# Five token tiles of a linear-attention and MLP kernel, set to other addresses in SBUF

## The chip, the cores and the metric

One core of one Trainium2 chip runs the whole kernel. The metric is device time in microseconds of one execution; the kernel before was run three times, and the median counts.

## What is computed

Linear attention on 4 x 8 heads of 576 tokens, then a gated MLP with an RMS norm ahead of it, then a second MLP. The weights come in as 64-bit floats.

```python
def phi(x):                                   # random features, 128 of them
    h = einsum('bhsd,md->bhsm', x, omega) - sum(x * x, -1) / 2
    return exp(h - max(h, -1)) / sqrt(m)
q_p, k_p = phi(q * scale), phi(k * scale)
kv, z = einsum('bhsm,bhsd->bhmd', k_p, v), sum(k_p, axis=2)
x = einsum('bhsm,bhmd->bhsd', q_p, kv) / (einsum('bhsm,bhm->bhs', q_p, z) + 1e-6)
# (2304 tokens, 512)
xn = x / sqrt(mean(x * x, -1) + 1e-6) * rms_g
g = xn @ w_gate                               # 512 x 1536
x = (g * sigmoid(g) * (xn @ w_val)) @ w_out   # 1536 x 512
h = x @ w2_in                                 # 512 x 2048
return (h * sigmoid(h)) @ w2_out              # 2048 x 512
```

## The kernel before

**Tiles.** The 2304 tokens are 18 tiles of 128, taken in five blocks: four long ones of 512 tokens and a short one of 256 (`blocks`, L58). Block `j` has one token tile `xs[j]` (L91): for each of the 128 partitions, two halves (a high and a low part of each number, in fp32r) times four chunks of the 512 features times the block's tokens. A weight tile holds, in the same manner, a high and a low half of 512 columns. Every product is made of three passes (`PASS`, L236): high by high, high by low, low by high. `part` (L247) issues the matmuls of one product of a token block: 12 of them, with a weight slice of 128 columns as the stationary operand and a slice of `xs[j]` (512 or 256 columns) as the moving one. Its line is L250. Each matmul has a weight load of its own, which the trace lists as engine PEld.

**Order.** In the attention stage (up to about 190 us) a list written out by hand, `ORDER`, sets the order of all operations; it holds the first products of blocks 0 to 2, too (L250 into tiles named b, and L1067). After that `stream` (L357) runs eleven sweeps over the hidden columns, five of the first MLP and six of the second. In each sweep every block has its L250 products (tiles named g), and between them stand the products of the block ahead of it that lead back to 512 features: L304 in the first MLP (a weight slice stationary, the hidden tile `h` moving), L337 in the second (`h` stationary, a weight tile moving), both into tiles named y. So long g work and long y work take turns, and once in each sweep the short block comes in between.

**Addresses.** Tiles are laid out in SBUF one behind the other: constants, the five `xs` tiles, `ya`, weight tiles, and the rest, with another group of weight tiles at the far end (padded by `EDGE` elements, L185). A weight tile has 4,096 bytes in each partition, a long `xs` tile 16,384, a hidden tile 4,096 or 2,048. All of these are whole multiples of 512 bytes, and so all the weight tiles, hidden tiles and long token tiles begin at one and the same address modulo 512 (it is 192). The slices that a matmul takes are also multiples of 512 bytes into a tile. The word **offset** is used below for the moving operand's address less the stationary one's, modulo 512 bytes. Before, it is 0 for all L304 and L337 matmuls and for L250 of the long blocks, and 64 for L250 of the short block, whose tile is shifted by `SHIFT` = 16 elements of 4 bytes inside a longer buffer. In the attention stage L661 (the feature projection, `hl` stationary and `bd` moving, 256 columns) runs at offsets 384 and 416, as the buffers happen to lie.

**Others that touch the token tiles.** ScalarE and VectorE write them in the attention stage (L908, L956, L961), and in the fifth sweep, between the two MLPs, L317 and L294 write them anew.

Of the kernel before, what the change touches and what calls it, by code (L numbers as in the profile page):

```python
# [9 lines left out]
F32R = mybir.dt.float32r  # L10
# [10 lines left out]
def kernel(  # L21
# [20 lines left out]
    P = 128  # L42
    G = 4
    KC = DM // P
    TB = 4
    EDGE, SHIFT = 72, 16
    scale = 1.0 / float(D) ** 0.25
    half = -0.5 * scale * scale
    eps_den = 1e-6 * M
# [9 lines left out]
    NB, NE = len(blocks), 3  # L59
    tidx = {t: i for i, t in enumerate(tiles)}  # L60

    def out_rows(i):
# [10 lines left out]
    big = ctx.enter_context(tc.tile_pool(name="big", bufs=1))  # L73
# [14 lines left out]
    g_sb = const.tile([P, KC], F32)  # L88
    mhalf = const.tile([P, 1], F32)

    xs = [  # L91
        big.tile([P, 2 * KC * n + (0 if n == TB * P else 8 * SHIFT)], F32R, name=f"xs{j}")
        [:, (0 if n == TB * P else SHIFT):][:, 0:2 * KC * n].rearrange("p (a c n) -> p a c n", a=2, c=KC)
        for j, n in enumerate(blocks)
    ]
    ya = [big.tile([P, KC * blocks[j]], F32, name=f"ya{j}") for j in range(NE)]
# [9 lines left out]
    f = 0  # L106
# [4 lines left out]
    f = 0  # L111
# [978 lines left out]
    with tc.manual_schedule():  # L1090
# [62 lines left out]
        n = 0  # L1153
        for j in range(NE):
            n = add_block(j, sweeps[0][1], n)
# [52 lines left out]
```

## Time and profile before

| | |
|---|---|
| Median of three runs | 982.45 us (981.73 to 982.59) |
| Span of the profiled execution | 980.8 us |
| TensorE busy (PE) | 973.2 us, 99% of the span |
| VectorE, ScalarE, GpSimd busy | 59%, 40%, 30% |
| Chain that ended last | PE 96% |

The page gives the profiled execution's span, from its first to its last instruction, and no other total for it; the median of the runs is 1.7 us above it. TensorE is busy nearly all the time, and the chain of waits that ended last is nearly all its matmuls. The mean duration that the trace gives a matmul holds some 163 ns in which the next one is already streaming, so durations do not add up. What adds up is the time from one start to the next; the chain shows it, since a piece of the chain is a run of matmuls with its length and count.

### The profile page before, as it was taken

Reading aid. Unit: us, or ns where it says so; the run is one execution under the profiler, and the core shown is the slowest. Engines: PE = TensorE matmul, PEld = TensorE weight load, DVE = VectorE, ACT = ScalarE, POOL = GpSimd, SP = SyncE. Lnnn points to the kernel's source line nnn. Section 1 sums busy time; section 2 is a strip of 40 time slices with the busy share of each in tenths; the row PEclk is TensorE's granted clock in tenths of the full one; section 3 lists DMA queues with packets and bytes.
Section 4 is the critical chain, followed back from the end, with each engine's and each line's share of the span. In section 5 each row is a group of like instructions: output and inputs, shape, how many; then the busy total and the mean of one; then the engine's idle time right before and its main releaser. Section 6 shows DMA issues by size and latency. Waiting matters only on the chain.

```text
span 980.8 us, 15407 instructions
## 1 busy us (share of the span) xinstructions
PE 973.2 (99%) x5938; PEld 828.0 (84%) x5938; DVE 575.8 (59%) x1186; ACT 392.5 (40%) x904; POOL 291.3 (30%) x308
## 2 busy tenths in 40 slices
PE   9999999999999999999999999999999999999998
PEld 8989888888888888888898888888888888888887
DVE  7999999886532366774234873615634735435634
ACT  7999777753311123341113334443223223222221
POOL 8877653453310033341001322402402302202200
PEclk9999999999999999999999999999999999999999
DMA  8645443222200012221000111201101101100023
GB/s 197 161 103 139 122 115 114 73 88 74 77 22 1 1 43 65 87 86 44 1 1 22 56 54 43 65 22 43 65 22 43 65 22 43 43 1 22 22 86 108
DMA packets 79481, 60.31 MB, mean 61 GB/s; under 512 B 27312, under 2 KB 73648, under 8 KB 79408
## 3 DMA queue, kind: packets, MB, share of 16 engines
q1 hardware_dynamic: 79136, 59.26, 20.5%
q8 instruction: 47, 0.77, 0.3%
q14 instruction: 26, 0.21, 0.1%
q10 hardware_dynamic: 272, 0.07, 0.0%
HBM read 49.87 MB, written 4.72 MB: 56 GB/s over the span
## 4 chain that ended last, share of the span: by engine, by line
PE 96%; DVE 2%; ACT 1%; DMA 1%; issue 0%; POOL 0%; SPq 0%; ACTq 0%; DVEq 0%; POOLq 0%
PE g L250 46%; PE y L337 20%; PE y L304 13%; PE b L661 5%; PE b L250 3%; PE b L843 2%; PE kv L739 2%; PE b L1067 2%; PE b L632 1%; PE b L947 1%; PE b L819 1%; DVE small L678 0%; DMA x<-in_k_dram 0%; SPq L799 0%; ACT m L176 0%
## 5 line engine op out<-in xcount | busy, mean ns | idle before, releaser
L250 PE MATMUL g<-xs,w 128*128 128x512 f32 (+1 forms) x2256 | 468.0, 366 | 0.0
L250 PEld LDWEIGHTS g<-xs,w 128*128 128x128 f32 x2256 | 391.1, 188 | 70.1
L168 POOL TENSOR_TENSOR m<-m,raw 128x512 int32<-128x512 int32 x136 | 188.5, 1387 | 580.0 <-issue 415.4
L244 DVE TENSOR_TENSOR h<-s,h 128x512 fp32r<-128x512 f32 (+1 forms) x134 | 96.7, 722 | 185.2 <-ACT h L243 185.2
L337 PE MATMUL y<-w,h 128*128 128x512 f32 (+1 forms) x870 | 200.8, 388 | 0.0
L337 PEld LDWEIGHTS y<-w,h 128*128 128x128 f32 x870 | 162.2, 188 | 33.3
L243 ACT ACTIVATE h<-s 128x512 fp32r<-128x512 f32 (+1 forms) x134 | 78.7, 588 | 180.2 <-DVE s L273 158.2
L304 PE MATMUL y<-h,w 128*128 128x512 f32 (+1 forms) x648 | 135.5, 366 | 0.2 <-DVE h L244 0.2
L304 PEld LDWEIGHTS y<-h,w 128*128 128x128 f32 x648 | 112.2, 189 | 20.2 <-DVE h L244 0.4
L284 ACT ACTIVATE s<-g 128x512 f32<-128x512 f32 (+1 forms) x80 | 44.4, 556 | 171.1 <-PE g L250 171.0
L348 DVE TENSOR_TENSOR ya<-y,ya 128x512 f32<-128x512 f32 (+1 forms) x91 | 62.1, 683 | 57.9 <-PE y L337 56.6
L315 DVE TENSOR_TENSOR ya<-y,ya 128x512 f32<-128x512 f32 (+1 forms) x80 | 50.3, 635 | 58.3 <-PE y L304 58.1
L709 ACT ACTIVATE e<-b,nb 128x128 f32<-128x128 f32 x272 | 75.7, 401 | 14.0 <-DVE nb L691 5.4
L273 DVE TENSOR_TENSOR s<-s,g 128x512 f32<-128x512 f32 (+1 forms) x54 | 33.8, 626 | 77.5 <-PE g L250 76.1
L191 ACT ACTIVATE w<-m 128x512 fp32r<-128x512 f32 x68 | 42.8, 630 | 68.7 <-POOL m L168 67.5
L661 PE MATMUL b<-bd,hl 128*128 128x256 f32 x432 | 62.4, 289 | 0.7 <-DVE xt L870 0.5
L661 PEld LDWEIGHTS b<-bd,hl 128*128 128x128 f32 x432 | 55.1, 188 | 4.1 <-ACT e L709 0.8
L194 DVE TENSOR_TENSOR w<-m,w 128x512 fp32r<-128x512 f32 x68 | 53.9, 792 | 2.1 <-ACT w L191 1.9
L267 ACT ACTIVATE s<-g 128x512 f32<-128x512 f32 (+1 forms) x54 | 29.5, 546 | 59.0 <-PE g L250 58.9
L678 DVE TENSOR_REDUCE small<-b 128x4 f32<-128x512 f32 x72 | 49.8, 691 | 4.4 <-PE b L661 2.5
L585 POOL TENSOR_TENSOR sq<-sq 128x256 f32<-128x256 f32 (+2 forms) x80 | 45.7, 584 | 2.4
L581 POOL TENSOR_TENSOR sq<-x 128x512 f32<-128x512 f32 (+1 forms) x40 | 38.1, 959 | 27.3 <-DVE ns L594 10.6
(75 smaller groups left out, 725.5 us busy)
## 6 DMA issues: line engine op xcount, KB each, us to landing
raw<-in_moe_w_out_dram SPq DMA_DIRECT2D x28, 512.0 KB, 3.5
raw<-in_moe_w_in_dram SPq DMA_DIRECT2D x16, 512.0 KB, 3.7
raw<-in_moe_w_gate_dram SPq DMA_DIRECT2D x12, 512.0 KB, 3.7
raw<-in_moe_w_val_dram SPq DMA_DIRECT2D x12, 512.0 KB, 3.5
qT<-e SPq DMA_DIRECT2D x72, 64.0 KB, 2.2
x<-in_k_dram SPq DMA_DIRECT2D x16, 256.0 KB, 3.7
va<-in_v_dram SPq DMA_DIRECT2D x32, 128.0 KB, 4.0
x<-in_q_dram SPq DMA_DIRECT2D x16, 256.0 KB, 3.5
```

The lines of the kernel that those rows point to most:

```text
L168: tt(out=mi, in0=mi, in1=(low if step == 5 else high).bitcast(I32), op=ALU.add)
L194: nc.vector.tensor_tensor(out=st.t[:, 1, :], in0=st.m.bitcast(F32), in1=st.t[:, 0, :].bitcast(F32), op=ALU.subtract)
L243: nc.scalar.activation(out=ht[:, 0, :], in_=s, func=AF.Copy)
L244: nc.vector.tensor_tensor(out=ht[:, 1, :], in0=s, in1=ht[:, 0, :].bitcast(F32), op=ALU.subtract)
L250: nc.tensor.matmul(out=ps, lhsT=w[:, a, cc * P:(cc + 1) * P], rhs=xs[j][:, c, cc, :], start=(n == 0), stop=(n == 3 * KC - 1),)
L304: nc.tensor.matmul(out=ps, lhsT=wt[1, "o", f][:, a, d * P:(d + 1) * P], rhs=hs[f][:, c, :], start=(n == 0), stop=(n == nn - 1),)
L315: nc.vector.tensor_tensor(out=y[:, d, :], in0=ps, in1=y[:, d, :], op=ALU.add)
L337: nc.tensor.matmul(out=ps, lhsT=hs[f][:, a, t * P:(t + 1) * P], rhs=wt[2, "p", f][:, c, d0:d1], start=(n == 0), stop=(n == nn - 1),)
L348: nc.vector.tensor_tensor(out=o[:, t, d0:d1], in0=ps, in1=o[:, t, d0:d1], op=ALU.add)
L661: nc.tensor.matmul(out=st.ps[r][:, 2 * j:2 * j + 2, :].rearrange("p h m -> p (h m)"), lhsT=st.hl[:, c, 2 * r + j, :], rhs=bd[:, a, :], sta ...
L678: nc.vector.tensor_reduce(out=st.mx[:, G * r:G * r + G], in_=st.ps[r], axis=AX.X, op=ALU.max)
L709: nc.scalar.activation(out=st.e[r][:, :, h, :] if blocks4 else st.e[r][:, h, :], in_=src.rearrange("p (a f) -> p a f", a=4) if blocks4 els ...
```

## The change

Each token tile gets a lead of its own, in elements of 4 bytes: 16, 32, 16, 48 and 48. Since the tiles lie one behind the other, the leads add up: the long tiles come to lie 64, 192, 256 and 448 bytes past the weight tiles' address modulo 512, and the short one 640, which is 128. A tail of 96 elements behind the short tile brings the sum to 1,024 bytes, where there were 512 before; so all that lies behind the token tiles moves by 512 bytes and keeps its address modulo 512, and the weight tiles at the far end do not move at all. The offset of L250 is now 64, 192, 256 and 448 in blocks 0 to 3 and 128 in block 4. The offsets of L304, L337, L661 and L1067 stay as they were. No instruction is added, removed or moved: on each engine the list of instructions is the same row by row.

```diff
-    EDGE, SHIFT = 72, 16
+    EDGE = 72
...
+    LEAD, REST = (16, 32, 16, 48, 48), 96
     xs = [
-        big.tile([P, 2 * KC * n + (0 if n == TB * P else 8 * SHIFT)], F32R, name=f"xs{j}")
-        [:, (0 if n == TB * P else SHIFT):][:, 0:2 * KC * n].rearrange("p (a c n) -> p a c n", a=2, c=KC)
+        big.tile([P, 2 * KC * n + LEAD[j] + (REST if j == NB - 1 else 0)], F32R, name=f"xs{j}")
+        [:, LEAD[j]:][:, 0:2 * KC * n].rearrange("p (a c n) -> p a c n", a=2, c=KC)
         for j, n in enumerate(blocks)
     ]
```

## Rows read from the trace of the kernel before

**Rows 1.** The page: span, busy time by engine, granted clock, chain by engine and line.
```profile
span 980.8 us, 15407 instructions
PE 973.2 (99%) x5938; PEld 828.0 (84%) x5938; DVE 575.8 (59%) x1186; ACT 392.5 (40%) x904; POOL 291.3 (30%) x308
...
PEclk9999999999999999999999999999999999999999
...
PE 96%; DVE 2%; ACT 1%; DMA 1%; issue 0%; POOL 0%; SPq 0%; ACTq 0%; DVEq 0%; POOLq 0%
PE g L250 46%; PE y L337 20%; PE y L304 13%; PE b L661 5%; PE b L250 3%; PE b L843 2%; PE kv L739 2%; PE b L1067 2%; PE b L632 1%; PE b L947 1%; PE b L819 1%; DVE small L678 0%; DMA x<-in_k_dram 0%; SPq L799 0%; ACT m L176 0%
```
**Rows 2.** Groups of PE instructions by shape: busy us, mean ns | idle before.
```profile
L250 PE MATMUL g<-xs,w 128*128 128x512 f32 x1776 | 411.4, 389 | 0.0
L337 PE MATMUL y<-w,h 128*128 128x512 f32 x858 | 199.4, 389 | 0.0
L304 PE MATMUL y<-h,w 128*128 128x512 f32 x504 | 117.2, 389 | 0.0
L661 PE MATMUL b<-bd,hl 128*128 128x256 f32 x432 | 62.4, 289 | 0.7 <-DVE xt L870 0.5
L250 PE MATMUL g<-xs,w 128*128 128x256 f32 x480 | 59.8, 280 | 0.0
L250 PE MATMUL b<-xs,w 128*128 128x512 f32 x144 | 37.7, 399 | 0.4 <-DVE w L194 0.4
...
L304 PE MATMUL y<-h,w 128*128 128x256 f32 x144 | 18.3, 283 | 0.2 <-DVE h L244 0.2
```
**Rows 3.** Chain, 217 to 304 us: start us, length us, what. Long blocks alone.
```profile
217.36 16.35 PE g L250 x72
233.71 8.16 PE y L304 x36
241.87 16.32 PE g L250 x72
258.19 8.16 PE y L304 x36
```
**Rows 4.** Granted clock in such a stretch: PE busy (count), PEclk, DMA share, GB/s.
```profile
220.00:300.00 80.00, 80.00 (x355) 1.00 0.17 53
```
**Rows 5.** Chain, the short block's 256-column matmuls: L250 at offset 64, L304 at 0.
```profile
315.93 4.71 PE g L250 x40
...
324.82 3.12 PE y L304 x26
```
**Rows 6.** Chain, the seven long matmuls behind a short block.
```profile
307.26 1.62 PE y L304 x7
```
**Rows 7.** Chain, 640 to 800 us: long y work behind long and behind short g work.
```profile
701.34 8.16 PE y L337 x36
709.50 8.27 PE g L250 x48
717.76 8.20 PE y L337 x36
```
**Rows 8.** Chain, attention stage: L250 at offset 0, L661 at 384.
```profile
137.78 2.77 PE b L250 x12
...
151.18 1.43 PE b L661 x12
```
**Rows 9.** The token tiles' writers behind 189 us: count, duration ns min/median/max, first to last.
```profile
L317 ACT ACTIVATE xs<-ya x20: 417/632/635, 525.9 to 588.7; 128x512 fp32r<-128x512 f32 x16, 128x256 fp32r<-128x256 f32 x4
L294 DVE TENSOR_TENSOR xs<-ya,xs x20: 411/682/1161, 527.2 to 589.1; 128x512 fp32r<-128x512 f32 x16, 128x256 fp32r<-128x256 f32 x4
```

## The prediction, made before the changed kernel ran

> **What bounds the kernel now.** The page comes first: TensorE is busy 973.2 us of a span of 980.8, and the chain that ended last is 96% TensorE; L250 alone has 46% of it as g and 3% as b [rows 1]. The list of groups shows no idle time worth a name ahead of the matmuls of the sweeps [rows 2]. So the span is the sum of the times from one matmul's start to the next, and a change that moves no instruction counts only if it changes these. The groups' mean durations cannot be added, so I read the chain: a run of matmuls, its length and its count.
>
> In a long stretch, 72 matmuls of L250 take 16.32 us, 226.7 ns each, and the L304 matmuls next to them the same, 8.16 by 36 [rows 3]. The clock is granted in full there, 1.00 [rows 4], which is the 2.4 GHz level; 512 columns at 2.4 GHz would be 213.3 ns, so each long matmul carries 13.3 ns on top of its columns. In the short block there are two cases side by side with 256 columns, 106.7 ns: L304 at offset 0 takes 3.12 us by 26, 120.0 ns, and L250 at offset 64 takes 4.71 by 40, 117.8 ns [rows 5]. The surcharge is thus 13.3 ns at offset 0 whether the matmul is long or short, and 11.1 at offset 64. It belongs to the matmul with its weight load, not to the columns, and the address has a part in it. The same difference stands in the mean durations, 283 against 280 [rows 2].
>
> One more thing is to be seen in the chain, and it weighs more for me. The long matmuls' 226.7 ns is a steady rhythm, and they are dearer whenever they are out of it. Right behind a short block seven long matmuls take 1.62 us, 231.4 each [rows 6]. The whole piece of 36 then takes 8.20 where one behind long work takes 8.16 [rows 7]. In the attention stage, where other work cuts in all the time, twelve of L250 in a row take 2.77 us, 230.8 each [rows 8], and that group's mean duration is 399 against 389 [rows 2]. With 256 columns it is the other way about: the steady 120.0 at offset 0 is the dear one, and L661, cut up all the time and at offset 384, runs 1.43 by 12, 119.2 [rows 8].
>
> **The change part by part.** *Long tiles, offset 0 to 64, 192, 256 and 448.* This concerns 1776 matmuls of the sweeps [rows 2], 432 in each of blocks 0 to 2 and 480 in block 3; the 144 of the attention stage are out of rhythm already [rows 2, 8], and I take nothing for them. The trace has no long matmul at any offset but 0, so this cost is bounded. From above: the offset keeps the stream out of its cheap rhythm all the time, at the 230.8 to 231.4 that it shows when out of it [rows 6, 8], which is 4.1 to 4.7 ns more; 1776 x 4.2 = +7.5 us, 1776 x 4.7 = +8.3 us. From below: the long matmul gains what the short one has at 64 against 0, 2.2 ns [rows 5], 1776 x 2.2 = -3.9 us. Far below that, the whole surcharge of 13.3 ns goes, -23.6 us. I take +7.5, from the row of 512 columns and the longer run of the two (the twelve of L250), and not the gain of the 256-column rows. My reason: a 256-column matmul gives its weight load about as much time as its columns need, a long one twice that, and rows 6 and 8 show the two to differ in sign when the rhythm is disturbed.
>
> *Turns between g and y.* Now a turn from long g work to long y work costs nothing, 8.16 behind long and 8.20 behind short work [rows 7], both pairs of operands being at offset 0. With the g work at another offset I expect each such turn to cost what one behind the short block costs, 0.04 us. There are eleven sweeps by three long blocks whose y work lies between long g work, less the three blocks that the attention stage has done: 30 turns, +1.2 us. Lower bound: none of it.
>
> *Short tile, 64 to 128.* 480 matmuls at 117.8 ns [rows 2, 5]. Nothing shows offset 128; the nearest are 119.2 at 384 [rows 8] and 120.0 at 0 [rows 5]. I take nothing; the bounds are +2.2 ns x 480 = +1.1 us, and as much below.
>
> *ScalarE's and VectorE's work on the tiles.* Twenty instructions of each in the fifth sweep, about 0.63 and 0.68 us [rows 9], with TensorE never waiting for them [rows 2]. Ten per cent more on each would be under 0.1 us at a time, hidden behind the 8 us of long y work. Nothing. DMAs, semaphores and the order are untouched.
>
> **The sum.** +7.5 +1.2 = +8.7 us on a span of 980.8, 989.5; with the 1.7 us between span and median, 991.2 us.
>
> A rule that speaks against any effect: the Trainium skill, TensorE: Matmul & The Clock Gate, section Step-by-step: what each phase is for, says that TensorE reads the moving operand and the weights through two independent SBUF ports and that loading the next weights takes no read bandwidth from the running matmul. By that, addresses would not matter, and the sum would be zero: 982.4. The 2.2 ns between two 256-column streams that differ in offset [rows 5] do not fit it, though they differ in the tiles they read and write, too.
>
> **The rivals.** *A, the forecast:* 991.2 us. For it, rows 6 and 8. Against it: the out-of-rhythm stretches that I price it with are themselves at offset 0, so they show that the rhythm can be missed, not that another offset misses it. And four offsets may well come out four ways.
>
> *B, the gain of the short block carries over:* -3.9 +1.2 = -2.7 us, 979.7, and 978.5 if the turns cost nothing. This is the other sign, and one mechanism: at offset 0 the weight load for the next matmul and the moving operand walk through the same addresses modulo 512 and get into each other's way, and off it they do so less. Its place is every long L250 matmul; its price 2.2 ns; it decides once a long matmul comes out below 226.0 ns, since from there 1776 of them outweigh the turns. For it: rows 5, and the equal 13.3 ns at both lengths. Against it: rows 6 and 8, where a long stream that is out of step gets dearer.
>
> *C, nothing happens:* the start of the weight loads adapts itself to the moving stream, whatever the address, and the steady rhythm stays 226.7; with or without the turns 982.4 to 983.7. For it: L250, L304 and L337 agree to the nanosecond, 389 [rows 2], though their tiles lie far apart. Against it: rows 5. It is also what the page's rule named above gives.
>
> *D, some offsets free the stream of most of the surcharge:* all of it on all four tiles would be 982.4 - 23.6 = 958.8; on one or two of them, 965 to 975. Nothing in the trace shows a 512-column matmul under 226 ns for long, so this is a tail. The same page, in its section "Wait — 56ns, not 53.3ns?", gives 215.7 ns for a 512-column matmul back to back; an estimate from it is 11 x 1776 = 19.5 us less.
>
> **How the numbers follow.** A 0.50, B 0.25, C 0.14, D 0.11. The measurement tells about 0.2% from no change, 2 us: below 980.5 is faster, above 984.4 slower. Faster: D and 0.19 of B, 0.30. Within: the rest of B, 0.10 of C and 0.02 of A where offsets cancel, 0.18. Slower: 0.48 of A and 0.04 of C, 0.52. The likeliest case alone runs from 985 (half of the tiles keep the rhythm) to 997 (the dear end of 4.7 ns, +1.1 for the short tile, and some matmuls dearer than any row). As both signs hold much, the range goes from 975, which takes in B and C whole and leaves most of D out, to 998.
>
> **What would show it.** In the changed kernel's chain, pieces of L250 between y work of the same length: 72 in 16.3 us is C, 16.6 is A, 16.2 is B, under 16.0 is D. Since each block has its own offset, they may differ: block by block is the reading. The y pieces behind them at 8.20 instead of 8.16 show the turns. The short block: 40 in 4.71 if 128 is like 64. The mean duration of L250 with 512 columns goes to about 393 in A and 387 in B. What would make it wrong: long matmuls at a new offset that settle at a steady time under 226 ns, or TensorE idle ahead of y work, which would mean that another engine, not the matmuls, had changed.

## The result: 1.0% slower, by way of a second settled rhythm

The changed kernel takes 992.01 us (median of 3, 990.75 to 992.25) where the kernel before takes 982.45. The ratio is 1.0095, 95% interval 1.0077 to 1.0113. The forecast was 991.2 us, with a range of 975 to 998.

The page of the changed kernel (span; busy time by engine; granted clock) answers to [rows 1]:

```profile
span 990.4 us, 15407 instructions
...
PE 983.1 (99%) x5938; PEld 828.9 (84%) x5938; DVE 574.5 (58%) x1186; ACT 392.5 (40%) x904; POOL 291.6 (29%) x308
...
PEclk9999999999999999999999999999999999999999
```

The same instructions, the clock granted in full, and PE busy for 9.9 us more in a span 9.6 us longer. No group of PE's gained more than 0.5 us of idle time: PE itself takes longer for the same work. In the matmul groups by shape (busy us, mean ns | idle before), the answer to [rows 2]:

```profile
L251 PE MATMUL g<-xs,w 128*128 128x512 f32 x1776 | 419.6, 393 | 0.0
L338 PE MATMUL y<-w,h 128*128 128x512 f32 x858 | 200.0, 390 | 0.0
L305 PE MATMUL y<-h,w 128*128 128x512 f32 x504 | 117.4, 390 | 0.0
...
L251 PE MATMUL g<-xs,w 128*128 128x256 f32 x480 | 60.5, 282 | 0.0
```

All lines stand one number higher than before: L251 is L250 of before, L305 is L304, L338 is L337. L251's long matmuls hold 8.2 us more, from a mean of 389 to 393 ns; y has about 0.8 us more, the short g block 0.7.

The chain of waits of the changed kernel, 217.6 to 306 us (start us, length us, what and how many), beside [rows 3]:

```profile
217.76 16.80 PE g L251 x72
234.56 8.18 PE y L305 x36
242.74 16.74 PE g L251 x72
259.48 8.16 PE y L305 x36
267.64 16.40 PE g L251 x72
284.04 8.18 PE y L305 x36
```

The first piece is mostly block 0, whose token tile is now at offset 64, the second block 1 (192), the third block 2 (256). The first two take 0.45 and 0.42 us more than the 16.35 and 16.32 of before; the third takes 0.08 more. A piece is not one block, though: it holds 60 matmuls of the block named and then the first 12 of the next one, since the y work comes in behind the next block's first product. So the prediction's reading of one piece for one block does not hold, and the 0.08 us are twelve matmuls of block 3. I therefore cut the chain inside the pieces, well away from the turns. Four such cuts, one in each block (offsets 64, 192, 256, 448 in this order), one in the last twelve matmuls of the third piece (block 3 again), and one in the short block (offset 128):

```profile
218.93 12.13 PE g L251 x52
...
243.91 12.13 PE g L251 x52
...
269.00 12.01 PE g L251 x53
...
281.47 2.33 PE g L251 x10
...
293.85 12.37 PE g L251 x53
...
317.40 5.28 PE g L251 x44
```

That is 233.3, 233.3, 226.6 and 233.4 ns a matmul in the four blocks, 233.0 in the twelve, and 120.0 in the short block. So the long stream has at least two settled rhythms (a rhythm is here a time from start to start whose mean repeats over dozens of matmuls). Three of the four tiles went from 226.7 to 233.3, one stayed where it was, and the short one went from 117.8 to 120.0, which is what L304 took at offset 0 [rows 5]. Block 0 does not keep to one value: in the second MLP those of its matmuls that stand behind the short block's y work run at 229.0 ns, as in this cut:

```profile
667.40 4.81 PE g L251 x21
```

Summed block by block over the sweeps, from one matmul's start to the next: block 0 +1.97 us, block 1 +2.81, block 2 +0.20, block 3 +3.15, together +8.13; y +0.78; the short block +0.67. Together that is the 9.6 us that the span grew.

### The profile page after: what moved, and what is told of

The parts are those of the page before. It is cut to its first block, busy times and chain, and to the rows that moved or that the text cites. A ratio compares the mean times of both kernels' runs of the same rounds, so it can differ in the third digit from the quotient of the medians.

```text
span 990.4 us, 15407 instructions
## 1 busy us (share of the span) xinstructions
PE 983.1 (99%) x5938; PEld 828.9 (84%) x5938; DVE 574.5 (58%) x1186; ACT 392.5 (40%) x904; POOL 291.6 (29%) x308
## 4 chain that ended last, share of the span: by engine, by line
PE 96%; DVE 1%; ACT 1%; DMA 1%; POOL 0%; SPq 0%; issue 0%; ACTq 0%; DVEq 0%; POOLq 0%
PE g L251 47%; PE y L338 20%; PE y L305 13%; PE b L662 5%; PE b L251 3%; PE kv L740 2%; PE b L844 2%; PE b L1068 2%; PE b L633 1%; PE b L820 1%; PE b L948 1%; DMA x<-in_k_dram 0%; SPq L800 0%; ACT m L177 0%; DVE w L195 0%
## 5 line engine op out<-in xcount | busy, mean ns | idle before, releaser
L251 PE MATMUL g<-xs,w 128*128 128x512 f32 (+1 forms) x2256 | 476.9, 370 | 0.0
L251 PEld LDWEIGHTS g<-xs,w 128*128 128x128 f32 x2256 | 391.7, 188 | 77.9
L338 PE MATMUL y<-w,h 128*128 128x512 f32 (+1 forms) x870 | 201.5, 388 | 0.0
L338 PEld LDWEIGHTS y<-w,h 128*128 128x128 f32 x870 | 162.2, 188 | 34.1
L305 PE MATMUL y<-h,w 128*128 128x512 f32 (+1 forms) x648 | 135.7, 366 | 0.1
L305 PEld LDWEIGHTS y<-h,w 128*128 128x128 f32 x648 | 112.3, 189 | 20.5 <-DVE h L245 0.3
L316 DVE TENSOR_TENSOR ya<-y,ya 128x512 f32<-128x512 f32 (+1 forms) x80 | 50.4, 635 | 60.4 <-PE y L305 60.3
```

The source lines that it names most:

```text
L251: nc.tensor.matmul(out=ps, lhsT=w[:, a, cc * P:(cc + 1) * P], rhs=xs[j][:, c, cc, :], start=(n == 0), stop=(n == 3 * KC - 1),)
L305: nc.tensor.matmul(out=ps, lhsT=wt[1, "o", f][:, a, d * P:(d + 1) * P], rhs=hs[f][:, c, :], start=(n == 0), stop=(n == nn - 1),)
L316: nc.vector.tensor_tensor(out=y[:, d, :], in0=ps, in1=y[:, d, :], op=ALU.add)
L338: nc.tensor.matmul(out=ps, lhsT=hs[f][:, a, t * P:(t + 1) * P], rhs=wt[2, "p", f][:, c, d0:d1], start=(n == 0), stop=(n == nn - 1),)
```

## The experiments

In the diffs, LEAD is each token tile's lead in 4-byte words (blocks 0 to 3, then the short one), REST the filling behind the last. Blocks are told apart by the time of the cut: in the second long sweep they stand at about 331, 348, 365 and 381 us.

**Which offsets are dear.** Three versions of the changed kernel with other leads, each run once: long tiles at 32, 128, 320 and 384 and the short one at 448; at 16, 48, 96, 160 and 256; at 240, 288, 480, 496 and 192. (A tile's length is rounded up to whole 32 bytes, so a lead of 16 or 240 bytes moves the tiles behind it by 32 or 256.)

```diff
-    LEAD, REST = (16, 32, 16, 48, 48), 96
+    LEAD, REST = (8, 24, 48, 16, 16), 16
+    LEAD, REST = (4, 4, 8, 16, 24), 64
+    LEAD, REST = (60, 8, 48, 4, 48), 80
```

> Five other offsets in one run: blocks 0 to 3 at 32, 128, 320 and 384 bytes, the short block at 448. Theory P, the offset of the token tile to the weight tiles decides, with a period of 256 bytes: block 2 (320, like 64) settles at 233.3 ns for each long matmul, blocks 1 and 3 (128 and 384) agree with each other, at 226.7 or 233.3, and block 0 (32) lies at one of these two. Theory Q, a period of 512 bytes: 320 is new, and blocks 1 and 3 need not agree. Theory R, my forecast's own reason (a stream off offset 0 finds no steady rhythm and runs at a mean of about 231 ns): all four blocks at uneven spacings of 224 to 241 ns with a mean near 231. The short block at 448 (under P like 192) is not known: 117 to 122 ns.

> Small offsets: blocks 0 to 3 at 16, 48, 96 and 160 bytes, the short block at 256. Theory P (the offset decides, period 256): the short block at 256 runs like a 256-column matmul at offset 0, 120.0 ns. If what counts is only whether the offset is an exact multiple of 256, all four long blocks are at 233.3 ns; if it is how far the two operands lie apart, 16 stays at 226.7 and 96 and 160 are at 233.3. Theory R (no rhythm off offset 0): a mean near 231 ns with uneven spacings in all four.

> Long blocks at 240, 288, 480 and 496 bytes, the short one at 192. Theory P with exact multiples of 256 as the only cheap offsets for long matmuls: all four between 231 and 235 ns, like 16, 32 and 48 in an earlier run; the run near 995 us. If nearness to a multiple counts on the far side: 240 and 496 nearer to 226.7 than 288 and 480. The short block at 192 between 115 and 120 ns.

Measured: 992.54, 995.7 and 993.0 us, beside 982.4, 982.4 and 982.5 for the kernel before on the same chips. Cuts through the chain of the first version (long at 32, 128, 320 and 384; then the short block at 448, once right behind long g work and once behind y work):

```profile
331.43 6.77 PE g L251 x29
...
347.86 7.23 PE g L251 x31
...
364.96 6.18 PE g L251 x27
...
380.80 7.24 PE g L251 x31
...
307.39 2.15 PE g L251 x19
...
317.72 4.95 PE g L251 x42
```

Long: 233.4, 233.2, 228.9 and 233.5 ns. Short, at one and the same offset: 113.2 ns behind long g work and 117.9 behind y work. From the second version, offset 16 and the short block at 256, and from the third, offset 240:

```profile
331.48 6.72 PE g L251 x29
...
318.17 4.91 PE g L251 x41
```

```profile
328.99 8.04 PE g L251 x34
```

231.7, 119.8 and 236.5 ns (offset 240 has a mean of 234.9 over all sweeps). The others lie at 233 to 234: over the sweeps, 48, 96 and 160 have means of 233.3, 233.8 and 234.2, and 288, 480 and 496 of 233.5, 233.2 and 232.9. With the changed kernel's three that is fifteen offsets that are dearer than 226.7, by 2.2 to 10 ns; of all that were tried, 0 and 256 alone are cheap.

Of the theories, the period of 256 bytes holds in what is cheap, and 128 and 384 agree; but 320 did not come out like 64 in the changed kernel (228.9, not 233.3), and 16 came out at neither of its two forecast values. Theory R is wrong in its mean, since the four means of the first version are 233.5, 232.9, 229.5 and 233.1 ns and not 231, but right in that single spacings need not be even: at 128 they are 229 and 238 ns by turns, at 320 they are 226, 229 and 232, where the changed kernel at 64 mostly had 233 and 234. A rhythm off the cheap offsets is thus often a pattern that repeats, and the values given here are its means.

For 256 columns, 0 and 256 are the dear ones (120.0), as is 128; 64, 192 and 448 lie at 113 to 118. So the two lengths differ in sign at 0 and 256, which the prediction had from [rows 6, 8]; at 128 both are dear.

**The address itself, or the offset between the operands.** A 64-byte tile is put ahead of everything in the kernel before and the edge behind is cut as much, so that tokens, weights and hidden tiles all stand elsewhere and every offset of the sweeps stays.

```diff
-    EDGE, SHIFT = 72, 16
+    EDGE, SHIFT = 56, 16
...
+    skew = const.tile([P, 16], F32)
```

> The kernel before with 64 bytes put in ahead of the token tiles and the far group of weight tiles set 64 bytes on: token, weight and hidden tiles all lie at 256 modulo 512 instead of 192, and their offsets to each other are those of before. Theory P (the offset decides): long matmuls at 226.7 ns, short at 117.8, 982.4 us within 1. Theory A (the token tile's own address decides; in the changed kernel the long tile at 256 modulo 512 ran at 233.3 ns): 6.7 ns on 1776 matmuls, 994 us.

Measured: 981.63 us, ratio 0.999 (0.9981 to 1.0000). The chain:

```profile
233.15 8.16 PE y L305 x36
241.31 16.32 PE g L251 x72
```

To the hundredth the pieces of [rows 3]. Moving all operands together by 64 bytes is worth nothing, so the token tile's own address is not the cause: a long tile at 256 modulo 512 takes 226.7 ns here and 233.3 in the changed kernel. What is left is where the operands stand to each other.

**Weights alone moved.** In the kernel before, only the weight tiles go up by 64 bytes; tokens and hidden tiles stay.

```diff
-    EDGE, SHIFT = 72, 16
+    EDGE, SHIFT = 56, 16
...
+    wa.tile([P, 16], F32, tag="skew", name="skew", bufs=1)
...
+            back.append(rawp.tile([P, 112], F32, tag="skew1", name="skew1", bufs=1))
...
+            skewed.append(pool.tile([P, 16], F32, tag="skew2", name="skew2", bufs=1))
```

> The kernel before with all weight tiles set 64 bytes on and nothing else moved: token and hidden tiles stay at 192 modulo 512. Offsets now: 448 for long L250 and for all L304, 64 for L337 (there the weight tile is the moving operand), 0 for the short block's L250. Theory P (the two operands of a matmul against each other): 229 to 233.3 ns on all 1776 long L250 and all 1362 long y matmuls, +2.3 to +6.7 ns each, and 120 instead of 117.8 in the short block: +8 to +22 us, 990 to 1004 us. Theory T (what counts is where the token tiles lie against anything else than the weights): L250 stays at 226.7 ns, as its token tiles have not moved, and the time within 2 us of 982.4.

Measured: 999.64 us, ratio 1.0177 (1.0162 to 1.0192). L256 and L310 of this kernel (L250 and L304 of before) are then at offset 448, and L343 (L337), whose weights are the moving operand, at 64. Cuts of its chain:

```profile
218.81 12.37 PE g L256 x53
...
234.21 5.83 PE y L310 x25
...
654.24 8.24 PE y L343 x36
...
670.86 8.40 PE g L256 x36
679.26 8.39 PE y L343 x36
```

233.4, 233.2, 228.9, 233.3 and 233.1 ns (the two L343 pieces are at one offset). The tokens stood still, and their long matmuls pay the same 6.7 ns as in the changed kernel; and y, untouched by the change, pays it too. The theory of the token address alone falls, that of the two operands against each other stands, and the time lies in its range. The weights' own address is not the cause either, since the run before had them 64 bytes on, too, and lost nothing. The Trainium skill (TensorE: Matmul & The Clock Gate, Step-by-step: what each phase is for) has the moving operand and the weights read through independent ports, the load taking no read bandwidth from the running matmul. By that, 64 bytes on the weights should cost nothing. This run does not agree for 4-byte operands: it lost 1.8%. By what means the two operands get into each other's way, it does not show.

**Every long tile at the cheap offset.** The changed kernel with all four long tiles at 256 and the short one at 64, as before.

```diff
-    LEAD, REST = (16, 32, 16, 48, 48), 96
+    LEAD, REST = (64, 0, 0, 0, 80), 112
```

> All four long token tiles at offset 256, the short one at 64 as before. Theory P (the offset decides, 256 is as good as 0): 226.7 ns for each long matmul, no cost at turns between g and y work, 982.4 us within 1. Theory M (block 2 of the changed kernel was cheap because of its neighbours or its own address, not for its offset): blocks 0, 1 and 3 stay at 233.3 ns, about 991 us. Turns between streams of unequal offset cost 0.04 us each: 983.7 us.

Measured: 982.68 us, ratio 1.0002 (0.9993 to 1.0012). The chain:

```profile
217.56 16.35 PE g L251 x72
233.91 8.16 PE y L305 x36
242.06 16.32 PE g L251 x72
```

The whole loss is gone with the offsets, though no tile stands where it stood before. The turn to y at 8.16 shows something more: g at 256 hands over to y at 0 at no cost. So it is not unequal offsets as such that make a turn cost something; the turns that do cost stand behind streams of another rhythm.

**Every tile at one dear offset.** All five at 64.

```diff
-    LEAD, REST = (16, 32, 16, 48, 48), 96
+    LEAD, REST = (16, 0, 0, 0, 0), 112
```

> All five token tiles at offset 64. Theory P (the offset decides): 233.3 ns on all 1776 long matmuls, 1776 x 6.7 = 11.8 us, the short block as before at 117.8, and about 1 us for long y work that starts out of step behind g work: 982.4 + 12.8 = 995 us. Theory M (the four tiles at four different offsets got in each other's way): less than the changed kernel's +9.6 us.

Measured: 989.4 us, ratio 1.007 (1.0056 to 1.0083); it should have been 995. Cuts in block 0, in the first twelve matmuls of block 1, and in the rest of blocks 1 and 2:

```profile
218.92 12.13 PE g L251 x52
...
232.22 2.33 PE g L251 x10
...
243.92 12.13 PE g L251 x53
...
268.85 12.36 PE g L251 x54
```

233.3, 233.0, 228.9 and 228.9 ns at one and the same offset. Block 1's tile alone has both values in one sweep: its first twelve matmuls follow block 0's without a break and keep its rhythm, and the other sixty follow long y work. So the offset decides that the stream leaves 226.7, but not alone where it settles: what ran just before has a part in it. The short block of the first version above shows the same (113.2 and 117.9 at offset 448). Theory M had a loss below 9.6 us, too, and 6.9 came, but its reason does not fit: values near 229 also stand where the tiles lie at four different offsets (229.0 in block 0 of the changed kernel, 228.9 at 320 in the first version).

**The short tile alone.** Long tiles at 0 as before, the short one at 448 instead of 64.

```diff
-    LEAD, REST = (16, 32, 16, 48, 48), 96
+    LEAD, REST = (0, 0, 0, 0, 112), 16
```

> Long tiles at offset 0 as in the kernel before, the short one at 448, where a run with other offsets showed 115.8 ns. Theory P (the offset decides, block by block): 480 x 2.1 = 1.0 us less than before, 981.4 us, a ratio of 0.999, at the edge of what can be told. If the short block's gain hung on the long tiles' offsets in that run: 117.8 ns again and no change.

Measured: 981.56 us, ratio 0.999 (0.9981 to 0.9999): the forecast number, for another reason. The short block stayed at 117.8 ns, and that also where it stands right behind long g work, as in the first row below (118.0 ns). The first version above had 113.2 at the same place and offset, with the long g work ahead of it at 384 and not at 0; so the gain did hang on the long tiles, as the second theory has it. What was gained here lies behind the short block, as the other two rows show:

```profile
386.48 1.77 PE g L251 x15
...
644.17 8.16 PE y L338 x36
...
660.54 8.16 PE g L251 x36
```

These pieces are at 226.7 throughout; the 8.20 of [rows 7] behind a short block is gone. Summed, y has 0.4 us less and block 0 0.3 us.

**Half of each weight load.** If the weight load's reads stood in the matmul's way, loading half as many columns should take half of the surcharge away. Eleven of twelve L251 matmuls load 64 of 128 columns and make 64 rows of output; the other half of these products is left out.

```diff
+            m = P if n == 0 else P // 2
...
-                out=ps,
-                lhsT=w[:, a, cc * P:(cc + 1) * P],
+                out=ps[0:m],
+                lhsT=w[:, a, cc * P:cc * P + m],
...
+                skip_group_check=True,
```

> The changed kernel, with eleven of a product's twelve L251 matmuls loading 64 weight columns instead of 128 and filling half of the output's partitions: half of each product is left out there. Same count, same moving operands, same offsets (64, 192, 256, 448, short 128). Theory W (the surcharge on a matmul's columns is the weight load getting in the way of the moving stream): it shrinks with the load, for offset 256 from 13.3 ns to 6 to 8 (about 220 ns a matmul), and the 6.7 ns between 256 and the others to 2 to 4 ns. Theory S (a fixed cost of starting a matmul, that depends on its operand's address): 226.7 and 233.3 ns as before.

Measured: 990.56 us. A piece of the chain each from mostly block 0, 1 and 2 (64, 192, 256), and the weight loads by shape (busy us, mean ns of one | idle before):

```profile
218.56 16.48 PE g L252 x72
...
243.24 16.69 PE g L252 x72
...
268.10 16.57 PE g L252 x72
```

```profile
L252 PEld LDWEIGHTS g<-xs,w 128*64 128x64 f32 x2068 | 271.1, 134 | 148.8
```

A load does get shorter, 134 ns where the changed kernel has 188. Over the sweeps the blocks' means are 228.6, 232.0, 229.8 and, in block 3, 232.4 ns, where the changed kernel has 232.3, 233.2, 227.1 and 233.5. The surcharge over 213.3 ns does not halve, it stays at 15 to 19, so theory W falls in the form given. Theory S, the values of before, does not come out either: block 0 gets cheaper and block 2 dearer. So the load's width, or the halved output that goes with it, has a part in which rhythm settles.

**Half the bytes of both operands.** The changed kernel with the token, weight and hidden halves kept as bf16 in the same buffers. The tiles start where they did; the slices inside them are half as long, which puts half of the matmuls 256 bytes off those offsets. The halves carry fewer bits, so the result is coarser; columns, instructions and order are the same.

```diff
-        [:, LEAD[j]:][:, 0:2 * KC * n].rearrange("p (a c n) -> p a c n", a=2, c=KC)
+        [:, LEAD[j]:][:, 0:KC * n].bitcast(BF16).rearrange("p (a c n) -> p a c n", a=2, c=KC)
...
-        st.t = t[:, 0:2 * KC * P].rearrange("p (a n) -> p a n", a=2)
+        st.t = t[:, 0:KC * P].bitcast(BF16).rearrange("p (a n) -> p a n", a=2)
```

> The changed kernel with the token, weight and hidden halves held as bf16 instead of fp32r (its result is a little coarser, the halves carry fewer bits): same instructions on TensorE, same counts, same columns, same start addresses of the tiles, but half the bytes for each column and for each weight load. Theory W (the surcharge is the reading of the operands from SBUF: moving stream and weight load get into each other's way): nearly all of the 13.3 to 20 ns goes, 214 to 219 ns for 512 columns whatever the offset, so about 10 ns on 1362 y matmuls and 10 to 17 on 1776 of L251: 950 to 960 us. Theory S (a fixed cost of starting a matmul by its address): 226.7 and 233.3 ns stay, 992 us.

Measured: 939.37 us, ratio 0.9568 (0.9552 to 0.9585), which beats both kernels and lies below the forecast range. A line of its page, its groups of long g matmuls and of weight loads for L252, and two cuts of its chain (a long y piece, a short one):

```profile
PE 923.5 (99%) x5852; PEld 514.9 (55%) x5938; DVE 577.4 (62%) x1186; ACT 391.4 (42%) x904; POOL 290.4 (31%) x308
```

```profile
L252 PE MATMUL g<-xs,w 128*128 128x512 bf16 x1733 | 389.0, 379 | 2.2
...
L252 PEld LDWEIGHTS <-w 128*128 128x128 bf16 x2400 | 233.7, 98 | 230.0 <-DVE w L195 1.2
```

```profile
252.09 7.77 PE y L306 x36
...
314.34 3.93 PE y L306 x36
```

215.8 ns for 512 columns and 109.2 for 256: the columns' time and 2.5 ns. Start to start, g is at 215 to 216 ns in all four blocks, at 64, 192, 256 and 448 alike; the dependence on the offset is gone together with the surcharge. (The trace lacks some 2% of this kernel's matmul records, so counts of pieces in g are low.) PEld's busy time falls from 828.9 to 514.9 us, one load of L252 from 188 to 98 ns. 215.8 is what the Trainium skill gives for 512 columns (TensorE: Matmul & The Clock Gate, Wait — 56ns, not 53.3ns?, 215.7 ns): the trace agrees for bf16, and for the 4-byte operands of this kernel it does at none of the offsets tried.

The sum fits, too, and shows what the forecast range left out, the short block and the attention stage: 1776 long g matmuls from a mean of 231.6 to 215.8 are 28.1 us, 1362 long y from 227.5 to 215.8 are 15.9, the short block's 480 g and 144 y at 10 to 11 ns are 6.4: 50.4 of the 53.0 us by which the span is shorter. The rest lies in the attention stage; I did not part it. What this run does not tell apart is the bytes, the number format and the shorter load: all three changed at once.

## Why the prediction came out, and where its reason did not

- **What bounds the kernel:** right. The span is the sum of TensorE's start-to-start times; no wait grew, and all of the 9.6 us are found there. The chain was the view that told it, cut inside the pieces, since a piece mixes two blocks; the pieces came at 16.80, 16.74 and 16.40 us, none at the 16.6 of A. The group's mean told it rightly as well (393 forecast, 393 measured).
- **Long tiles, +7.5 us; measured +8.1:** the size is right, the reason is not. The step that failed is the price's ground: that the offset "keeps the stream out of its cheap rhythm all the time, at the 230.8 to 231.4", on all 1776. In its place there is a second settled rhythm at 233.3 ns on most of the 1344 matmuls of three tiles, and none of it on the 432 of block 2. 1344 x 6.7 = 9.0 us; the sums of these three give 7.9, since they stood at 0.6 us above their rhythm before (block 0 at 98.4 us where 432 x 226.7 is 97.9) and now, with part of block 0 near 229, at 0.4 below it. Dearer per matmul and on fewer of them: two errors that cancel, so the size came out by luck. That "four offsets may well come out four ways" stood in the text as an objection; it was the better guess.
- **B, the gain of the short block:** did not occur. With 4-byte operands no long matmul settled under 226.6 ns at any of the offsets tried. That the two lengths differ in sign held at 0 and 256, where 256 columns are dear and 512 cheapest, and not at 128.
- **C, nothing happens:** falls with the three tiles at 233.3, and again with the weights moved alone, which made the kernel 1.8% slower. It holds for one tile of five, the one at 256.
- **D:** none of the offsets tried frees the stream of the surcharge. The bf16 halves bring it from 13.3 ns at best to 2.5.
- **Turns, +1.2 us; measured +0.8:** the mechanism (y needs time to get back to its rhythm) is right; the term was too large, since a turn behind long g work costs between nothing and 0.04 us, not 0.04 throughout. In the chain of the changed kernel at 675 to 733 us:

```profile
675.23 8.20 PE y L338 x36
...
691.77 8.16 PE y L338 x36
...
708.17 8.18 PE y L338 x36
...
724.81 8.21 PE y L338 x36
```

  What runs right ahead of these pieces is the next block's first product: block 1 (192) ahead of the first, which costs 0.04, block 2 (256) ahead of the second, which costs nothing, block 3 (448) ahead of the third, which costs 0.02. The fourth stands behind the short block, where 0.04 was paid before, too. The cause named, other offsets of g, is not quite it: g at 256 costs y nothing (so also in the version with all at 256).
- **Short tile, 0 within 1.1; measured +0.7:** 128 is not like 64 but, most of the time, like 0 (120.0 for 117.8).
- **Writers and DMAs, nothing:** right; PE's idle times are those of before within 0.5 us a group.

Term by term the sum missed +0.6 us on the long tiles, -0.4 on the turns and +0.7 on the short block: 9.6 where it had 8.7.

Still open: what makes the surcharge. Halving the load's columns left it, bf16 in both operands took most of it away; nothing here changed one operand alone, or the bytes without the number format. Nor does a run tell a matmul's own weights from those that are loaded for the next one, as all weight tiles share one address modulo 512. Open too: why 0 and 256 are the cheap offsets, and what in the work before a stretch picks its rhythm.

## What to carry to other kernels

Where the chain is nearly all TensorE, read it as start-to-start time per matmul and stretch by stretch; a value that stays the same over fifty matmuls is a rhythm, and a layout change can move a stream from one to another (here 226.7 to 233.3 ns). With 4-byte operands, keep a long matmul's moving and stationary operand at the same address modulo 256 bytes, and measure anew for another number of columns, since 256 columns liked other offsets. Do not price a state that no row shows by one that is merely near: a transient's price (231 ns) came near here by luck.

## What the runs showed of the hardware that was not expected

- A stream of 512-column matmuls with 4-byte operands settles at one of several means, among them 226.7, 228.9, 231.7, 233.3 and 236.5 ns, start to start, at one granted clock of 1.00 throughout; one of 256 columns at 113.2, 117.8 or 120.0.
- Sixteen nonzero offsets between the operands were tried on long g matmuls; 256 alone costs nothing. 16 bytes are enough to cost 5 ns.
- The same offset gives two rhythms depending on what ran before: 233.3 and 228.9 at 64, 117.9 and 113.2 with 256 columns at 448, and 118.0 there when the long work ahead lies at 0.
- With bf16 operands of the same columns the surcharge falls to 2.5 ns, from 13 to 23, and it is the same at every offset that run has.
